# A planned attention-and-gate kernel: due times worked back from TensorE, one block fewer in plain float32, one tap a block by DMA

## The chip, the cores and the metric

The kernel runs on one core of one Trainium2 chip. The metric is the device time of one execution, in microseconds (us). The engines are called PE (TensorE, the matrix engine), DVE (VectorE), ACT (ScalarE), POOL (GpSimd) and SP (SyncE, which only issues DMAs here).

## The reference

Attention without a softmax, then a gated projection, all in float32:

```python
batch, n_heads, seq, head_dim = (8, 12, 448, 64)

def _attn_ref(q, k, v):
    scores = scale * np.matmul(q, k.transpose(0, 1, 3, 2)) - np.log(S)
    attn = 1.0 / (1.0 + np.exp(-scores))
    return np.matmul(attn, v)

def _moe_ref(x, w_val, conv_w, w_out):       # x: batch, seq, 768, the heads side by side
    for k in range(5):
        gate_pre += conv_w[k] * xp[:, k:k + S, :]   # xp: x with 4 zero tokens ahead
    gate = 1.0 / (1.0 + np.exp(-gate_pre))
    val = x @ w_val
    return gate * val @ w_out
```

## The kernel before

**Tiles.** A pair is two heads of one batch, six pairs a batch, 48 in all; a block ("two" in the code) is two pairs, 24 in all, three blocks a batch. For each pair PE makes the scores in three chunks of 128 keys (`scores`, L516), and for each block the scores of the 64 keys that are left of each head (`scores_rest`, L539). ACT takes the sigmoid (L552). Then PE multiplies with the values (`attend`, L602 for the rest, L610 for the chunks). Columns of the result are the model's 768 columns in six groups of 128, a pair each. The tokens of the first batch (number 0) are handed out over the seven others as extra columns (448 + 64 = 512), so that the projections (`product`, L753) run for seven batches: for each of six column groups 18 matmuls of 512 columns, first with `w_val`, and later with `w_out`.

**Two ways of multiplying.** In plain float32 a matmul needs no preparation. In the split way both sides are cut into a high and a low half and three products are added. For the product with the values, blocks in `WHOLE` go in plain float32: the sigmoid is written straight to SBUF as `a_single`. The other blocks are split: after the sigmoid, which is left in PSUM, ACT writes a scaled float16 copy (L367, tile `a`) and DVE subtracts it from the PSUM tile (L563); the values are scaled by a power of two of their largest element (`vm` at L531, a small matmul with ones at L536, exponents at L544 and L573 to L577) and cut into `v_hi` and `v_lo` (L583). Score tiles lie in a ring of three in PSUM (`ps_a`), projection results in a ring of two (`ps_m`). Scores have a set of their own, `WHOLE_SCORES`, the first 15 pairs.

**The gate.** For each block of batches 1 to 7 the result `x` (L661 copies the edges, L658 takes its maximum for the scaling of its own split, `xs`) is multiplied by five taps. The first product writes `gate` (L367 on ACT or L369 on DVE). Each of the four others is either a multiply-add on DVE (L679), or a product on ACT into `tap` that a DMA issued by POOL adds into `gate` (L683). The last `ADDED` taps of each block go by DMA, in the first gated batch `ADDED_FIRST`; both column groups of a block have a product each and share the DMA. Then ACT takes the sigmoid (L685).

**Weights.** The 12 column groups of both matrices come as 64-bit words in two 32-bit halves and are converted in place (`convert`, L387, L389, L367 or L369; L412), measured (L415), summed over the partitions on PE (L421) and cut into `w_hi` and `w_lo`. Three word buffers are in flight.

**The largest x.** After a batch's last block, `x_largest` puts its column maxima on a diagonal (ACT) and spreads it over the partitions by two small matmuls (L702). These are written into the first score chunk of the block's second pair, as more matmuls ahead of the chunk's own.

**What sets the order.** All work is first listed as operations (`Plan.op`): the engines that may do it, each with a modelled cost (`ways`), a time `prio`, its inputs and outputs, and what must follow it at once (`then`). `Plan.issue` walks over a modelled clock: whenever an engine is free, it takes the ready operation with the smallest `prio`, in the order P, A, V, G, S of the engines. An operation with two ways is left to ACT if ACT is free within `AT["share"]` of the time. SP's and POOL's DMAs are listed the same way, with a modelled rate and delay. The `prio` times come from the table `AT` of some 45 numbers. The result is one fixed list, and the instructions are emitted in it, so that each engine runs its own in that order.

## Time and profile before

| | us |
|---|---|
| median of 3 runs (lowest, highest) | 579.44 (578.79, 579.93) |
| the profiled execution | 579.76 |
| its span, first to last instruction | 578.0 |
| PE busy | 571.4 |
| VectorE busy | 428.4 |
| ScalarE busy | 435.4 |
| GpSimd busy | 138.2 |

The granted clock of PE is 1.00 of full speed, 2.4 GHz, over the whole span. Busy times are the union of an engine's instructions; the end of a matmul is modelled, so that the time of a group of matmuls is better read from its start to the start of what comes next.

### The profile page before, as it was taken

The page shows a single profiled execution, that of the slowest core. Times are in us where ns is not written, and L with a number is a line of the kernel's source. Part 1 is how long each engine was busy: PE and PEld are TensorE (multiplying, and loading weights), DVE is VectorE, ACT ScalarE, POOL GpSimd, SP SyncE. Part 2 cuts the span into 40 slices and gives each one's busy share as a digit, 9 for nine tenths or more (in the row PEclk, how much of TensorE's full clock was granted, in tenths as well). Part 3 has the DMA queues.
Part 4 walks back from the last instruction along what each step waited for, and adds up shares of the span by engine and source line. Part 5 has one row for each costly group of instructions (what it writes and reads, how often), then busy time and mean ns, then how long its engine had stood idle before and what let it go on. Part 6 is the DMA issues. An engine that isn't in the chain of part 4 may idle for free.

```text
span 578.0 us, 9459 instructions
## 1 busy us (share of the span) xinstructions
PE 571.4 (99%) x3592; PEld 280.2 (48%) x3592; DVE 428.4 (74%) x693; ACT 435.4 (75%) x579; POOL 138.2 (24%) x162
## 2 busy tenths in 40 slices
PE   9999999999999999999999999999999999999997
PEld 5343334455555555545555454554545555544444
DVE  1867999899977959888598886889777886760310
ACT  5677988879888869778697878788788897862112
POOL 0000203332424222243322333223322322110000
PEclk9999999999999999999999999999999999999999
DMA  8988677757484564825657364565635663355012
GB/s 327 355 279 267 174 210 188 203 120 184 124 215 83 146 157 141 207 58 155 136 158 176 102 169 96 166 156 155 169 74 168 155 133 74 72 128 129 2 37 74
DMA packets 39310, 88.44 MB, mean 153 GB/s; under 512 B 14944, under 2 KB 20448, under 8 KB 39264
## 3 DMA queue, kind: packets, MB, share of 16 engines
q0 software_dynamic: 8640, 31.46, 29.4%
q1 hardware_dynamic: 30624, 56.37, 28.9%
q8 instruction: 28, 0.46, 0.3%
q14 instruction: 18, 0.15, 0.1%
HBM read 43.96 MB, written 12.40 MB: 98 GB/s over the span
## 4 chain that ended last, share of the span: by engine, by line
PE 90%; DVE 5%; ACT 3%; DMA 1%; issue 1%; ACTq 0%; DVEq 0%
PE ps_m L753 54%; PE ps_a L516 15%; PE ps_a L610 14%; PE ps_a L539 3%; PE ps_a L602 2%; DMA gate<-tap 1%; ACT a_single L552 1%; DVE x_max L658 1%; DVE gate L679 1%; PE ps_m L800 1%; DVE a L563 1%; DVE w_words L389 1%; DVE out_max L415 0%; ACT tap L367 0%; ACT a L367 0%
## 5 line engine op out<-in xcount | busy, mean ns | idle before, releaser
L753 PE MATMUL ps_m<-g,w_out_hi 128*128 128x512 f16 (+1 forms) x516 | 150.5, 374 | 0.0
L753 PE MATMUL ps_m<-xs,w_val_hi 128*128 128x512 f16 x504 | 150.1, 379 | 0.0
L552 ACT ACTIVATE ps_a<-ps_a 128x896 f32<-128x896 f32 x112 | 99.3, 909 | 14.2 <-DVE v_exp L544 6.5
L563 DVE SCALAR_TENSOR_TENSOR a<-ps_a,a 128x896 f16<-128x896 f32 x96 | 100.8, 1082 | 7.0 <-ACT a L367 6.7
L372 POOL TENSOR_TENSOR qk_lo<-qk_src,qk_hi 128x448 fp32r<-128x448 f32 x66 | 75.2, 1151 | 119.8 <-ACT qk_hi L361 36.7
L753 PE MATMUL ps_m<-g,w_out_lo 128*128 128x512 f16 (+1 forms) x258 | 96.5, 374 | 0.0
L683 POOL DMA_DIRECT2D gate<-tap x60 | 53.5, 892 | 178.6 <-ACT tap L367 70.2
L753 PE MATMUL ps_m<-xs,w_val_lo 128*128 128x512 f16 x252 | 95.5, 379 | 0.0
L367 ACT ACTIVATE a<-ps_a 128x896 f16<-128x896 f32 x96 | 85.0, 927 | 0.2
L367 ACT ACTIVATE tap<-x,cw 128x512 f32<-128x512 f32 x120 | 82.2, 739 | 1.5 <-DMA gate<-tap 1.5
L753 PEld LDWEIGHTS <-w_out_hi 128*128 128x128 f16 x516 | 49.0, 98 | 59.6 <-issue 5.3
L753 PEld LDWEIGHTS <-w_val_hi 128*128 128x128 f16 x504 | 47.8, 98 | 61.1 <-issue 5.9
L777 DVE SCALAR_TENSOR_TENSOR y<-ps_m,y_scale,gate 128x512 f32<-128x512 f32 x42 | 29.9, 745 | 34.3 <-PE ps_m L753 34.3
L610 PE MATMUL ps_a<-a,v_hi 128*64 128x448 f16 x384 | 52.7, 354 | 0.0
L367 ACT ACTIVATE y<-ps_m,o_scale 128x512 f32<-128x512 f32 (+1 forms) x35 | 23.1, 678 | 38.0 <-PE ps_m L753 25.4
L552 ACT ACTIVATE a_single<-ps_a 128x896 f32<-128x896 f32 x56 | 48.0, 927 | 4.5 <-PE ps_a L516 4.1
L361 ACT CAST g<-y 128x512 f16<-128x512 f32 x28 | 17.2, 618 | 33.7 <-DVE y L777 32.9
L516 PE MATMUL ps_a<-qk_hi 64*128 64x448 f32 x198 | 39.8, 398 | 0.1
L753 PEld LDWEIGHTS <-w_out_lo 128*128 128x128 f16 x258 | 25.2, 98 | 29.2
L753 PEld LDWEIGHTS <-w_val_lo 128*128 128x128 f16 x252 | 24.7, 98 | 29.7
L516 PE MATMUL ps_a<-qk_single 64*128 64x448 f32 x180 | 39.0, 566 | 0.0
L610 PE MATMUL ps_a<-a_single,v_src 128*64 128x448 f32 x192 | 37.8, 543 | 0.0
(108 smaller groups left out, 752.9 us busy)
## 6 DMA issues: line engine op xcount, KB each, us to landing
gate<-tap POOLq DMA_DIRECT2D x60, 512.0 KB, 4.9
qk_src<-qk SPq DMA_DIRECT2D x33, 448.0 KB, 5.4
v_src<-vs SPq DMA_DIRECT2D x24, 448.0 KB, 4.3
out_t<-y SPq DMA_DIRECT2D x41, 224.0 KB, 3.1
qk_single<-qk SPq DMA_DIRECT2D x15, 448.0 KB, 5.9
w_words<-w_val SPq DMA_DIRECT2D x6, 768.0 KB, 8.1
w_words<-w_out SPq DMA_DIRECT2D x6, 768.0 KB, 5.4
x<-first_x SPq DMA_DIRECT2D x21, 68.0 KB, 4.2
```

What stands on the lines that cost most here:

```text
L361: nc.scalar.copy(to, x)
L367: nc.scalar.activation(to, x, AF.Copy, scale=by)
L372: engines[eng].tensor_tensor(to, x, y, op=ALU.subtract)
L516: mm(b()[:, h, :S], k()[rows, at : at + P], q()[rows, :S], start=(n == 0), stop=(n == len(terms(i)) - 1))
L539: mm(b()[to, h, :S], x[n]()[rows, CW:], x[n]()[rows, :S], start=True, stop=True)
L552: nc.scalar.activation(to, b()[:, :, :S], AF.Sigmoid, bias=-math.log(S), scale=1.0 / math.sqrt(D))
L563: op({"V": 1.0}, t + 0.5, lambda e: nc.vector.scalar_tensor_tensor(part(1), p(), A_SCALE, part(0), op0=ALU.mult, op1=ALU.subtract), [b], [ ...
L602: mm(px()[to, p, :S], v()[rows, h * D : (h + 1) * D], x(s["a"])[rows, h, at : at + S], start=(j > 0 and n == 0), stop=(j == 0 and n == len ...
L610: mm(px()[to, p, :S], v()[:, o : o + D], x(st[2 * j + p]["a", c])[:, h, at : at + S], start=(j == 0 and c == 0 and n == 0), stop=(j > 0 an ...
L683: op({"G": 1.1}, at + AT["tap_step"] * k, lambda e, tap=tap: nc.gpsimd.dma_start(g(), tap(), accum_op=ALU.add), [tap], [g], 4 * P * T * 4, "")
L753: mm(po()[:, cs], w()[:, c, :], x(k)[:, cs], start=(c == 0 and j == 0), stop=(c == NC - 1 and j == 2))
L777: op({"V": 0.66}, t + AT["y"], lambda e: nc.vector.scalar_tensor_tensor(y(), po(), y_scale()[:, m : m + 1], gate()[:, m % 2, :], op0=ALU.m ...
```

## The change

Five things change. `WHOLE` is the first 7 blocks, not 8 (14 pairs for 16), so that block 7 goes the split way. `ADDED_FIRST` and `ADDED` are 1: of each block only the last tap goes by DMA. The first step of the weight words' conversion may run on ACT too, which reads the upper 16 bits of the low half and scales them. For batch 1 the spread of the largest x stands ahead of the third score chunk, not the first. And `issue` calls the old walk (now `order`) four times: after each, `deadlines` gives each operation but PE's a new `prio`, the latest start by which PE's operations could start without a gap in the order just made; the order whose last operation ends first on the modelled clock is emitted.

```diff
-WHOLE = {*range(8)}
+WHOLE = {*range(7)}
...
+TO_THREE_BITS = 7.498 / 2**16
...
-ADDED_FIRST = 2
-ADDED = 3
+ADDED_FIRST = 1
+ADDED = 1
+
+
+TIMES = 4
...
-    def issue(self):
+    def order(self):
...
+    def issue(self):
+
+
+        best = None
+        for n in range(TIMES):
+            order = self.order()
+            end = max(o.start + o.ways[o.eng] for o in order)
+            if best is None or end < best[0]:
+                best = end, [(o, o.eng, o.start, o.end) for o in order]
+            self.deadlines(order)
+        for o, o.eng, o.start, o.end in best[1]:
+            pass
+        return [o for o, *_ in best[1]]
+
+    def deadlines(self, order):
+
+
+        nexts = [[] for _ in self.ops]
+        for o in self.ops:
+            for d in o.deps:
+                nexts[d.n].append(o)
+            for d in o.after or ():
+                nexts[d.n].append(o)
+        due, t = {}, 0.0
+        for o in order:
+            if o.eng == "P":
+                due[o.n] = t = max(t, 0.0)
+                t += o.ways["P"]
+        last = t
+        for o in reversed(order):
+            cost = min(o.ways.values()) + (o.size / self.DMA_RATE + self.DMA_DELAY if o.size else 0.0)
+            at = due.get(o.n, last)
+            for x in nexts[o.n]:
+                at = min(at, x.due - (0.0 if o in (x.after or ()) else cost + self.HOP[o.eng]))
+            o.due = at
+        for o in order:
+            if o.eng != "P":
+                o.prio = o.due
+            o.start = o.end = None
...
-        op({"V": 0.06 + 0.41 * c}, prio, lambda e: nc.vector.tensor_scalar(
-            low(), low().bitcast(U32), 2.0**-29, 7.0, op0=ALU.mult, op1=ALU.min), [], [t])
+        op({"V": 0.06 + 0.41 * c, "A": 0.1 + 0.7 * c} if w is not cw_words else {"V": 0.1}, prio, lambda e: nc.vector.tensor_scalar(
+            low(), low().bitcast(U32), 2.0**-29, 7.0, op0=ALU.mult, op1=ALU.min) if e == "V" else scaled(
+            e, low(), w().bitcast(U16)[:, :, 1], TO_THREE_BITS), [], [t])
...
-    def score(i, after=None, sums=(), then=()):
-        first, middle, last = (scores(i, c, sums if c == 0 else ()) for c in range(3))
+    def score(i, after=None, sums=(), then=(), at=0):
+        first, middle, last = (scores(i, c, sums if c == at else ()) for c in range(3))
...
-            score(2 * j + 3, None, sums, then)
+            score(2 * j + 3, None, sums, then, 2 if j == 5 else 0)
```

## Rows read from the trace of the kernel before

**Rows 1.** Page, part 1: busy time, share of the span and instructions of each engine.

```profile
PE 571.4 (99%) x3592; PEld 280.2 (48%) x3592; DVE 428.4 (74%) x693; ACT 435.4 (75%) x579; POOL 138.2 (24%) x162
```

**Rows 2.** Chain that ended last, by time: start us, us, what; float32 block, split block.

```profile
109.42 0.75 PE ps_a L602 x8
110.18 4.66 PE ps_a L610 x24
...
160.81 0.57 PE ps_a L602 x12
161.38 3.53 PE ps_a L610 x36
...
166.93 7.88 PE ps_m L753 x36
```

**Rows 3.** PE timeline: start us, us, line, operation; the matmul of a block's largest values.

```profile
134.50 0.17 PE L536 MATMUL ps_a<-vm,ones 128*128 128x1 bf16 x1
134.59 0.98 PE L539 MATMUL ps_a<-qk_src 64*64 64x448 f32 x8
```

**Rows 4.** PE timeline before 142 us; in brackets idle time before and its releaser.

```profile
45.42 0.98 PE L539 MATMUL ps_a<-qk_single 64*64 64x448 f32 x8 [0.30 <-ACT a_single L552]
...
63.32 2.53 PE L516 MATMUL ps_a<-qk_single 64*128 64x448 f32 x12
...
74.69 2.80 PE L516 MATMUL ps_a<-qk_single 64*128 64x448 f32 x12
...
78.51 0.22 PE L702 MATMUL ps_a<-diagonal,ones 128*128 128x64 bf16 x2 [0.91 <-ACT diagonal L367]
...
81.68 0.59 PE L539 MATMUL ps_a<-qk_single 64*64 64x448 f32 x2 [0.39 <-ACT a_single L552]
...
139.91 0.36 PE L516 MATMUL ps_a<-qk_hi,qk_lo 64*128 64x448 f32 x2
140.11 0.36 PE L516 MATMUL ps_a<-qk_lo,qk_hi 64*128 64x448 f32 x2
140.58 0.47 PE L516 MATMUL ps_a<-qk_hi 64*128 64x448 f32 x2
```

**Rows 5.** Timeline of all engines at 76 to 79 us: the maximum and the diagonal.

```profile
76.62 1.21 DVE L658 TENSOR_REDUCE x_max<-x 128x2 f32<-128x1024 f32 x1
...
78.06 0.40 ACT L367 ACTIVATE diagonal<-eye,x_exp 128x128 bf16<-128x128 bf16 x1
```

**Rows 6.** Busy time of each engine in two stretches (header: the columns).

```profile
core 0: us, PE busy (x) PEld busy (x) DVE busy (x) ACT busy (x) POOL busy (x), PEclk, DMA share, GB/s
...
74.00:112.00 38.00, 36.69 (x203) 15.31 (x200) 35.78 (x68) 33.37 (x46) 9.41 (x12) 1.00 0.77 197
...
142.00:500.00 358.00, 358.00 (x2378) 184.33 (x2377) 291.12 (x450) 296.68 (x397) 109.04 (x118) 1.00 0.57 139
```

**Rows 7.** Groups of instructions over the span: busy us, mean ns | idle before.

```profile
L563 DVE SCALAR_TENSOR_TENSOR a<-ps_a,a 128x896 f16<-128x896 f32 x96 | 100.8, 1082 | 7.0 <-ACT a L367 6.7
...
L367 ACT ACTIVATE a<-ps_a 128x896 f16<-128x896 f32 x96 | 85.0, 927 | 0.2
L367 ACT ACTIVATE tap<-x,cw 128x512 f32<-128x512 f32 x120 | 82.2, 739 | 1.5 <-DMA gate<-tap 1.5
...
L683 POOL DMA_DIRECT2D gate<-tap x60 | 53.5, 892 | 178.6 <-ACT tap L367 70.2 <-DVE gate L679 29.6 <-ACT y L367 21.5
...
L387 DVE TENSOR_SCALAR w_words<-w_words 128x768 int32<-128x768 uint32 x12 | 7.5, 625 | 11.2 <-DMA w_words<-w_val 11.2
```

**Rows 8.** Groups of VectorE from 74 to 112 us.

```profile
L679 DVE SCALAR_TENSOR_TENSOR gate<-x,cw,gate 128x512 f32<-128x512 f32 x9 | 6.6, 742 | 0.0
...
L583 DVE SCALAR_TENSOR_TENSOR v_lo<-v_src,v_exp,v_hi 128x896 f16<-128x896 f32 x1 | 1.2, 1152 | 0.4 <-ACT v_hi L367 0.4
...
L531 DVE TENSOR_REDUCE vm<-v_src 128x1 bf16<-128x896 f32 x1 | 1.1, 1074 | 0.0
```

**Rows 9.** Who waited for whom over the span: us, times, longest us.

```profile
ACT x L367 <- PE ps_a L610: 27.0, 16, 2.5
```

More of the change, by code (lines that the diff above doesn't have):

```diff
@@ L17 @@
 I16 = mybir.dt.int16
+U16 = mybir.dt.uint16
 I64 = mybir.dt.int64
@@ L124 @@
 class Op:
-    __slots__ = ("ways", "prio", "emit", "deps", "n", "start", "end", "eng", "after", "size", "port", "then")
+    __slots__ = ("ways", "prio", "emit", "deps", "n", "start", "end", "eng", "after", "size", "port", "then", "due")
     def __init__(self, n, ways, prio, emit, size, port):
@@ L823, in score @@
         for f in then:
-            f(st[i]["ps", 0])
+            f(st[i]["ps", at])
         for c in range(3):
```

## The prediction

> **What bounds the kernel now.** I read the page's busy shares first. TensorE (PE) is busy for 99% of the span, VectorE (DVE) 74%, ScalarE (ACT) 75% [rows 1]. A busy share alone can hide bubbles, so next I read the chain that ended last in order of time. The reader is to see that from 142 us on it is made of PE pieces alone, each starting where the one before it ends, and that equal work takes equal time: one projection group of 36 matmuls takes 7.88 us at every place, one split attention-times-values takes 0.57 + 3.53 us [rows 2]. The table of stretches says the same: between 142 and 500 us PE is busy for 358.00 of 358 us, while DVE has 291 and ACT 297 [rows 6]. So after 142 us only the amount of PE work counts, and no other engine's saving can be seen in the time.
>
> Before 142 us it is different. The PE timeline has gaps there: 0.30 us at 45.4, 0.91 at 78.5, 0.39 at 81.7; two more delays lie inside pieces, seen in their lengths: 2.80 us where the same group takes 2.53, so 0.27 us at 74.7, and a step of 0.47 us at 140.1 where its like before it in the pattern take 0.20, so another 0.27 [rows 4]. Together 2.14 us. That is all that a better order of the other engines could win, whatever it does. The stretch that makes them is crowded: from 74 to 112 us DVE is busy 35.78 of 38 us and ACT 33.37 [rows 6].
>
> The head (30 warming matmuls, first load) and the tail (last eviction and store) are not touched.
>
> **The change, part by part.**
>
> One block fewer in plain float32 (WHOLE from 8 to 7 blocks of two pairs; the block with number 7). On PE the block's product with the values takes 0.75 + 4.66 us in float32 and 0.57 + 3.53 us as three float16 products [rows 2]: 5.41 - 4.10 = 1.31 us saved. The split form also needs one matmul with the largest values, which takes 134.59 - 134.50 = 0.09 us [rows 3]. Net -1.22 us. This lies on PE at 110 us, and everything behind it is a PE chain, so it comes off the end in full.
>
> What that costs elsewhere: seven score tiles of the block now need, after the sigmoid, a scaled copy on ACT (0.93 us each) and a subtraction on DVE (1.08 us each) [rows 7]: 6.5 us more on ACT and 7.6 us more on DVE. The block's values need a maximum (1.07 us), a low half (1.15 us) [rows 8], some 0.6 us of small exponent steps, and a high half of about 1 us on either engine. In all about 10.4 us on DVE and 7.5 us on ACT. All of it falls due between 80 and 112 us, where the block is multiplied.
>
> One tap a block by DMA (ADDED_FIRST 2 to 1, ADDED 3 to 1). The 3 blocks of batch 1 lose one DMA tap each, the 18 of batches 2 to 7 two each: 39 software DMAs of 60 go, each of which held GpSimd for 0.89 us, and 78 tap products of 0.74 us leave ACT [rows 7] and come back as 78 multiply-adds of 0.74 us on DVE [rows 8], in sum 58 us moved from one engine to the other. GpSimd's own work besides is the low halves of q, k and a few g and some memsets, so it only gets freer. After 142 us DVE has 67 us free of 358 [rows 6] and PE waits for nothing; an operation that may go on either engine is given to DVE only while ACT is taken, and ACT is relieved by as much as DVE is loaded. I cost it at nothing there; the cover is the 67 us free on DVE (18 blocks with 4 products of 0.74 us, 53 us, fall there at most, which fill it to 96% if nothing moves over) and the 61 us free on ACT plus what the taps leave. Were that cover gone, the evictions of the two projection buffers would be late first, and each late eviction stops PE. Before 120 us, for batch 1's gates, 6 products move: 4.5 us to DVE, as much from ACT.
>
> Weight words: the first of three conversion steps may now run on ACT. The trace of before has no such operation. The nearest ACT row of that size takes 0.93 us [rows 7], DVE takes 0.63 [rows 7]; strided 16-bit reading could double ACT's, or cost nothing. It is a choice, not a must, and lies beside PE's work: I take it as neutral, with 0.3 us either way in the range.
>
> The move of the column spread (the small matmuls that take the largest x of batch 1 over all partitions, from the first to the third score chunk). Before, PE came to them at 77.6 and waited until 78.51 for the diagonal on ACT, which waited for the maximum on DVE (76.62 to 77.83) [rows 4, 5]. Two of the three chunks of a group of 2.53 us [rows 4] now stand ahead, 1.69 us, more than the wait of 0.91. So this wait goes, -0.91 us, with 0.78 us to spare.
>
> Orders made anew. The order on every engine is static: the plan lists the operations with a modelled clock, and each engine runs its list as written. Now a due time is worked back for each operation from the time at which PE needs its result, the list is made again, four times in all, and the one with the earliest modelled end is kept. SP's loads and stores and GpSimd's subtractions are sorted by the same times, so the loads of weights fall behind loads of q, k and v that are due sooner. The other four delays (0.30 + 0.27 + 0.39 + 0.27 = 1.23 us) are of the kind that it can remove: at 45.4 and 81.7 PE waits for a sigmoid on ACT [rows 4], and ACT and DVE had work in hand that PE wanted later. At best all go, at worst they stay. I take 1.0 us as gone.
>
> New waits from the crowding. The added work before 112 us is 10.4 + 7.5 = 17.9 us on DVE and ACT together (the taps only change sides); from 74 to 112 us both together have 2.2 + 4.6 = 6.8 us free [rows 6]. If nothing could be put off, 11.1 us are left over, half of it on each engine, and PE would be late by 5.6 us. If enough can be put off, 0. Of the nine tap multiply-adds in that stretch [rows 8] several belong to gates whose projection groups come on PE only after 112 us, and so do the taps of batch 2 on ACT and the preparation of the last output weights; I estimate some 15 us of such work on both engines, a fifth of the 69 us that they do there [rows 6]. With 6.8 + 15 us of room against 17.9 that is nearer to full cover than to none: 0.6 us is what I take.
>
> Sum: -1.22 - 0.91 - 1.0 + 0.6 = -2.5 us. The profiled execution took 579.76 us, its span 578.0 and 1.76 around it; 579.76 - 2.5 = 577.2. The median of the runs, 579.44, is 0.32 below the profiled one, so 576.9.
>
> Not all idle time is usable. Over the whole span ACT stood 27.0 us, 16 times, before the copy of a block's result out of PSUM, waiting for PE while later sigmoids were queued behind that copy [rows 9]. The Trainium skill (Perfetto Trace Analysis, section Tensor Engine Instruction (MATMUL, LD_WEIGHTS)) says that ACT, DVE and GpSimd are strict FIFOs: an operation that waits holds all behind it. It speaks against this change, since a list made with modelled durations then pays for every error of the model; if for that reason none of ACT's free time were usable, an estimate by this rule puts PE 2.3 us later and the time at 579.2. The trace agrees with the rule in these 16 waits, but after 142 us they cost PE nothing.
>
> **The rivals.**
>
> (a) The order wins nothing: the same waits come back at other places, or the first order, by the old times, is the one kept. Then only the PE work counts, and each old wait goes for a new one of its size or up to double: 579.44 - 1.22 = 578.2, and up to 2.2 more, 580.4; say 579. For it: the DVE row of 74 to 112 us, 94% full before the change. Against it: the waits of before are few and small, and the biggest is removed by the move.
>
> (b) VectorE becomes the bound between 74 and 120 us. The place is the split of block 7's score tiles: the subtraction on DVE frees the PSUM tile, and three tiles are all there are, so a late subtraction stops the scores that follow. It decides from the point where less than 9 of the 17.9 us can be put off: then over 17.9 - 6.8 - 9 = 2.1 us are left, 1 us of PE, which eats what the order saves. With ACT's 4.6 us unusable, as in the waits of [rows 9], and 7.5 of the 15 us put off, 17.9 - 2.2 - 7.5 = 8.2 us are left. Shared by both engines that is 4.1 us of PE, 579.44 - 1.22 - 0.91 + 4.1 = 581.4; with all of it on DVE 585.5; say 582.5, nearer to the shared one. For it: DVE's added 10.4 + 4.5 us against 2.2 us free. Against it: the work that isn't due.
>
> (c) All old waits go and no new one comes: 579.44 - 1.22 - 2.14 = 576.1; under this the change has nothing to win save hidden delays of less than 0.5 us, so 575.6 is the floor.
>
> **How the numbers follow.** The forecast, 576.9, with waits between 0 and 2.2 us left over (576.1 to 578.2), has 0.55, the floor case (c) among it with 0.15; rival (a), 578.2 to 580.4, 0.22; rival (b), above 580.4, 0.20; something below 575.6, 0.03. A measurement of this kernel tells about 0.2% (1.2 us) from no change: below 578.3 is faster, above 580.6 slower. Faster 0.59, the same 0.21, slower 0.20. For 8 in 10 the range leaves out the far half of (b) and the few below the floor: 575.6 to 582.0.
>
> **What would show it.** PE's chain of the block at 110 us: 0.57 + 3.53 us instead of 0.75 + 4.66 (right for the first term). The spread's matmuls without a gap before them (right for the second). PE gaps before 142 us: their sum below 1.2 us is right for the order; gaps of a microsecond before scores or value products between 80 and 125 us, released by a DVE subtraction, would show (b). 358 of 358 us busy after 142 us again, with DVE at about 90% or flexible work gone over to ACT; any gap before a projection group there, released by an eviction, would prove the tap step wrong. The number of software DMAs must be 21. What would make the prediction wrong most easily is a model whose durations are off in the crowded stretch: the list is static, so it can't give way.

## The result and the profile after

The changed kernel takes 581.21 us (median of 11 runs, 580.46 to 583.22) against 579.44 for the kernel before on the same chip (11 runs, 578.79 to 580.10). The ratio is 1.0041, with a 95% interval of 1.0030 to 1.0052: slower by 0.4%, where 576.9 us was forecast. Four of the eleven executions are a group of their own: 582.9 to 583.2 us at a mean granted clock of 0.996, the other seven 580.5 to 581.3 at 0.999 or 1.000; the profile below is one of the seven (580.56 us, span 578.8). So the medians lie 1.8 us apart and the two profiled executions 0.8: the one before was 0.32 above its median, this one 0.65 below. Line numbers are 46 or 47 higher than before: the subtraction L563 is now L610, the projection L753 is L800, the scores L516 are L563.

Busy shares, from the page, as in [rows 1]; under it two groups of instructions that answer to [rows 7]:

```profile
PE 569.1 (98%) x3609; PEld 280.7 (48%) x3609; DVE 453.3 (78%) x735; ACT 425.4 (74%) x552; POOL 115.2 (20%) x129
...
L610 DVE SCALAR_TENSOR_TENSOR a<-ps_a,a 128x896 f16<-128x896 f32 x102 | 107.0, 1082 | 10.5 <-ACT a L413 10.5
...
L730 POOL DMA_DIRECT2D gate<-tap x21 | 18.6, 887 | 126.9 <-ACT ps_a L599 24.4
```

PE is busy for 2.3 us less than before and the span is 0.8 us longer: PE is rid of the work that it was to lose, and waits instead. (About 1.1 of the 2.3 us is block 7's product; 1.0 is the head, below.) There are 21 software DMAs and 102 subtractions, as the change says.

The table of stretches, as in [rows 6]:

```profile
core 0: us, PE busy (x) PEld busy (x) DVE busy (x) ACT busy (x) POOL busy (x), PEclk, DMA share, GB/s
74.00:112.00 38.00, 37.00 (x231) 17.08 (x229) 37.98 (x63) 34.08 (x46) 9.97 (x11) 1.00 0.46 128
112.00:142.00 30.00, 28.07 (x191) 14.81 (x190) 29.28 (x57) 27.48 (x36) 7.32 (x6) 1.00 0.36 106
142.00:240.00 98.00, 97.33 (x650) 49.83 (x649) 90.45 (x144) 81.72 (x108) 24.18 (x28) 1.00 0.42 109
240.00:500.00 260.00, 260.00 (x1725) 133.93 (x1724) 223.90 (x349) 200.64 (x260) 62.94 (x63) 1.00 0.34 93
```

From 74 to 112 us VectorE is busy for 37.98 of 38 us, before it was 35.78. PE loses 1.00 us there, 1.93 us between 112 and 142 us, 0.67 between 142 and 240, and nothing from 240 to 500. Who PE waited for, over the whole span (us, times, longest; left out is the 1.1 us before its first matmul, which the kernel before has too):

```profile
PE ps_a L563 <- DVE a_rest L610: 2.6, 2, 1.9
...
PE ps_a L749 <- ACT diagonal L413: 0.6, 1, 0.6
PE ps_a L583 <- DVE vm L578: 0.4, 1, 0.4
PE ps_a L586 <- ACT a_single L599: 0.3, 1, 0.3
```

The first line is two waits with one releaser, the subtraction of a split block's rest tile, which frees a PSUM tile of the ring of three for the scores that follow. This is the PE timeline at the first of them; block 7 is ahead of it, now as three float16 products:

```profile
107.51 0.56 PE L649 MATMUL ps_a<-a_rest,v_hi 64*64 64x448 f16 x8
...
108.18 0.57 PE L657 MATMUL ps_a<-a,v_hi 128*64 128x448 f16 x4
...
111.71 0.47 PE L563 MATMUL ps_a<-qk_hi 64*128 64x448 f32 x2
...
112.22 0.36 PE L563 MATMUL ps_a<-qk_lo,qk_hi 64*128 64x448 f32 x2
114.51 0.47 PE L563 MATMUL ps_a<-qk_hi 64*128 64x448 f32 x2 [1.93 <-DVE a_rest L610]
...
115.02 0.37 PE L563 MATMUL ps_a<-qk_lo,qk_hi 64*128 64x448 f32 x2
115.23 0.36 PE L563 MATMUL ps_a<-qk_hi 64*128 64x448 f32 x2
```

From start to start, block 7 takes 0.67 + 3.53 us (before 0.75 + 4.66, [rows 2]). Then the step from one score matmul to the next takes 114.51 - 112.22 = 2.29 us, where the same step takes 115.23 - 115.02 = 0.21: 2.08 us lost. What VectorE and GpSimd did meanwhile, from their timelines:

```profile
110.09 1.91 DVE L436 TENSOR_SCALAR w_words<-w_words 128x768 int16<-128x768 int16 x2
111.77 1.68 DVE L418 TENSOR_TENSOR g<-y,g 128x512 f16<-128x512 f32 x1
113.38 1.08 DVE L610 SCALAR_TENSOR_TENSOR a_rest<-ps_a,a_rest 128x896 f16<-128x896 f32 x1
...
111.06 1.85 POOL L418 TENSOR_TENSOR g<-y,g 128x512 f16<-128x512 f32 x1 [0.97 <-ACT g L407]
```

The subtraction that PE wants stands behind the low half of a `g` that PE wants later. That low half took 1.68 us, and GpSimd made another low half beside it. The 23 of its kind on VectorE after 142 us take 0.70 on average:

```profile
L418 DVE TENSOR_TENSOR g<-y,g 128x512 f16<-128x512 f32 x23 | 16.0, 698 | 0.2
```

The second wait is built alike and comes 125 us later. The lines show the high half of an `xs` on VectorE, two low halves of q and k on GpSimd, then the chain that follows on VectorE and ScalarE, and what PE lost:

```profile
226.69 3.38 DVE L415 TENSOR_SCALAR xs<-x,x_exp 128x1024 f16<-128x1024 f32 x1
...
227.11 2.39 POOL L418 TENSOR_TENSOR qk_lo<-qk_src,qk_hi 128x448 fp32r<-128x448 f32 x2
...
236.57 0.14 DVE L591 TENSOR_SCALAR v_exp<-ps_a 128x1 int32<-128x1 int32 x1
...
236.74 0.90 ACT L599 ACTIVATE ps_a<-ps_a 128x896 f32<-128x896 f32 x1 [1.78 <-DVE v_exp L591]
...
238.62 1.09 DVE L610 SCALAR_TENSOR_TENSOR a_rest<-ps_a,a_rest 128x896 f16<-128x896 f32 x1 [1.47 <-ACT a_rest L413]
...
238.73 0.36 PE L563 MATMUL ps_a<-qk_lo,qk_hi 64*128 64x448 f32 x2
239.77 0.47 PE L563 MATMUL ps_a<-qk_hi 64*128 64x448 f32 x2 [0.68 <-DVE a_rest L610]
```

3.38 us where the other three of its kind on VectorE take about 0.75 (minimum 736 ns, median 746 of the four). VectorE runs without a gap from there to the exponent step at 236.57; the sigmoid on ScalarE waits 1.78 us for that step, the rest subtraction for the copy behind the sigmoid, and PE for the subtraction: its step takes 239.77 - 238.73 = 1.04 us, 0.84 over the usual 0.2, and PE goes on 9.7 us behind the end of the long operation (230.07).

Where the span's +0.8 us comes from: block 7 and its small matmul -1.12; waits that are new, 2.08 at 112 us, 0.84 at 239 and 0.42 at 80; waits that are gone, 0.33 of the spread's, 0.39, 0.27 and 0.27 of [rows 4]; so waits +2.1. The tail is 0.65 longer: from the start of the last matmul to the end of the span 4.05 us before, 4.70 after. The head is 1.0 shorter, by chance (last section). Together +0.6; the rest is in small pieces.

### The profile page after: what moved, and what is told of

It reads as the page before. It is cut to its first block, busy times and chain, and to the rows that moved or that the text cites. A ratio compares the mean times of both kernels' runs of the same rounds, so it can differ in the third digit from the quotient of the medians.

```text
span 578.8 us, 9418 instructions
## 1 busy us (share of the span) xinstructions
PE 569.1 (98%) x3609; PEld 280.7 (48%) x3609; DVE 453.3 (78%) x735; ACT 425.4 (74%) x552; POOL 115.2 (20%) x129
## 4 chain that ended last, share of the span: by engine, by line
PE 85%; DVE 10%; ACT 2%; issue 1%; DMA 1%; ACTq 0%; DVEq 0%
PE ps_m L800 53%; PE ps_a L563 14%; PE ps_a L657 12%; PE ps_a L586 3%; PE ps_a L649 2%; DVE a L610 2%; DVE gate L726 1%; DVE xs L779 1%; DVE w_words L436 1%; DVE xs L415 1%; ACT a_single L599 1%; DMA w_words<-w_out 1%; PE ps_m L847 1%; DVE a_rest L610 1%; DVE x_max L705 0%
## 5 line engine op out<-in xcount | busy, mean ns | idle before, releaser
L800 PE MATMUL ps_m<-g,w_out_hi 128*128 128x512 f16 (+1 forms) x516 | 150.5, 374 | 0.2 <-ACT y L413 0.2
L800 PE MATMUL ps_m<-xs,w_val_hi 128*128 128x512 f16 x504 | 150.1, 379 | 0.0
L610 DVE SCALAR_TENSOR_TENSOR a<-ps_a,a 128x896 f16<-128x896 f32 x102 | 107.0, 1082 | 10.5 <-ACT a L413 10.5
L418 POOL TENSOR_TENSOR qk_lo<-qk_src,qk_hi 128x448 fp32r<-128x448 f32 x66 | 78.7, 1224 | 176.1 <-DVE qk_hi L409 120.9
L599 ACT ACTIVATE ps_a<-ps_a 128x896 f32<-128x896 f32 x119 | 105.0, 906 | 11.3 <-DVE v_exp L591 5.9
L800 PE MATMUL ps_m<-g,w_out_lo 128*128 128x512 f16 (+1 forms) x258 | 96.5, 374 | 0.0
L800 PE MATMUL ps_m<-xs,w_val_lo 128*128 128x512 f16 x252 | 95.5, 379 | 0.0
L726 DVE SCALAR_TENSOR_TENSOR gate<-x,cw,gate 128x512 f32<-128x512 f32 x126 | 91.4, 744 | 0.0
L413 ACT ACTIVATE a<-ps_a 128x896 f16<-128x896 f32 x102 | 89.8, 928 | 0.1
L800 PEld LDWEIGHTS <-w_out_hi 128*128 128x128 f16 x516 | 49.0, 98 | 59.9 <-issue 5.6
L800 PEld LDWEIGHTS <-w_val_hi 128*128 128x128 f16 x504 | 47.8, 98 | 61.1 <-issue 5.9
L407 ACT CAST g<-y 128x512 f16<-128x512 f32 x38 | 23.6, 620 | 51.3 <-DVE y L824 51.0
L413 ACT ACTIVATE y<-ps_m,o_scale 128x512 f32<-128x512 f32 (+1 forms) x43 | 28.2, 683 | 40.7 <-PE ps_m L800 26.9
L599 ACT ACTIVATE a_single<-ps_a 128x896 f32<-128x896 f32 x49 | 41.9, 928 | 3.7 <-PE ps_a L563 3.1
L730 POOL DMA_DIRECT2D gate<-tap x21 | 18.6, 887 | 126.9 <-ACT ps_a L599 24.4
L563 PE MATMUL ps_a<-qk_hi 64*128 64x448 f32 x198 | 40.0, 400 | 2.6 <-DVE a_rest L610 2.6
L800 PEld LDWEIGHTS <-w_out_lo 128*128 128x128 f16 x258 | 25.2, 98 | 29.2
L800 PEld LDWEIGHTS <-w_val_lo 128*128 128x128 f16 x252 | 24.7, 98 | 29.7
L563 PE MATMUL ps_a<-qk_single 64*128 64x448 f32 x180 | 37.6, 552 | 0.0
L563 PE MATMUL ps_a<-qk_hi,qk_lo 64*128 64x448 f32 x198 | 36.3, 362 | 0.0
```

Of the source, the lines that this page charges most:

```text
L407: nc.scalar.copy(to, x)
L413: nc.scalar.activation(to, x, AF.Copy, scale=by)
L418: engines[eng].tensor_tensor(to, x, y, op=ALU.subtract)
L563: mm(b()[:, h, :S], k()[rows, at : at + P], q()[rows, :S], start=(n == 0), stop=(n == len(terms(i)) - 1))
L599: nc.scalar.activation(to, b()[:, :, :S], AF.Sigmoid, bias=-math.log(S), scale=1.0 / math.sqrt(D))
L610: op({"V": 1.0}, t + 0.5, lambda e: nc.vector.scalar_tensor_tensor(part(1), p(), A_SCALE, part(0), op0=ALU.mult, op1=ALU.subtract), [b], [ ...
```

## The experiments

Three readings of the waits stood against each other. Theory A: the order of the list is bad in single places; each place can be mended alone, and the gains add. Theory B: VectorE is too full between 74 and 112 us as a whole; a wait mended in one place comes back in another. Theory C: VectorE and GpSimd share an access to SBUF, single operations of VectorE are stretched beside GpSimd's, and these make the waits. For the spread of the times, theory 1 puts it on the moment at which TensorE's clock rises in the head, theory 2 on a clock that falls again after a long gap.

In the edits, `move(n, x)` takes operation n out of the list that the plan made and puts it ahead of operation x; with 1 behind it, it puts it behind x. Nothing else in the list changes. Edits are against the changed kernel (`after`). The name in brackets is the run's.

**The changed kernel again (`after_again`).** No edit.

> The changed kernel once more, unedited. In its first eleven executions 7 took 580.5 to 581.3 us and 4 took 582.9 to 583.2 with a lower mean granted clock. Theory 1 (the head): TensorE's clock goes up at a different moment of the first microseconds from execution to execution, and an execution of the longer kind has the first score groups at the lower level for some 4.6 us more, which costs 2.3 us; its waits after 10 us are the same. Theory 2 (the gap): the longer kind comes from the wait of 1.9 us at 112 us, after which the clock falls. Both kinds should be seen again; a profile of the longer kind would have its low clock before 10 us (theory 1) or after 112 us (theory 2).

Measured: 581.31 us (580.79 to 583.44, 7 runs), ratio 1.0037 (1.0022 to 1.0053). Two of the seven are of the longer group (583.44 and 583.18, clock 0.996). The wait at 112 us is there again, 1.90 us. The head's 24 first score matmuls took 5.27 us here and 4.71 in the first profile of the same kernel, which is theory 1's part. In all profiles they differ by 1.1 us at most, and the longer group takes some 2 us more. No execution of that group was profiled.

**Block 8's rest subtraction ahead of the low half (`rest_first`).**

```diff
+    move(673, 557)
```

> The changed kernel with its list kept but for one place: on VectorE the subtraction of block 8's rest tile, which frees the score tile for which TensorE waits at 112 us, stands ahead of the low half of g, which stood ahead of it. Theory A (the order of the list): the wait of 1.93 us falls by the 1.5 us of the low half that stood in front, to 0.3 to 0.6 us, and the time by 1.2 to 1.6 us. Theory B (VectorE is too full as a whole): VectorE has no free time before 116 us, so the work put back stops TensorE a little later; the wait moves, and the time falls by less than 0.5 us. Theory 2 of the gap expects the longer kind of executions to be gone, theory 1 of the head expects as many of them.

Measured: 580.37 us (579.39 to 581.22, 11 runs), ratio 1.0016 (1.0007 to 1.0025), none of the longer group. The wait at 112 us in two parts, from the PE timeline of this kernel:

```profile
114.14 0.47 PE L563 MATMUL ps_a<-qk_hi 64*128 64x448 f32 x2 [0.35 <-DVE a_rest L610]
115.49 0.47 PE L563 MATMUL ps_a<-qk_hi 64*128 64x448 f32 x2 [0.47 <-ACT x L413]
```

1.93 us became 0.35, and 0.47 came up behind it, released by ScalarE. So this place made most of the wait, and some late work was hidden behind it: the time fell by 0.8 us, less than theory A's 1.2 to 1.6 and more than B's 0.5. The move did a second thing. The subtraction now runs beside GpSimd's low half at its usual length (1.09 us), and VectorE's low half, behind it, takes 0.67 us for 1.68. So 1.0 of the 1.68 us that stood in front was theory C's.

**The high half of xs behind two subtractions (`xs_later`).**

```diff
+    move(1091, 1087, 1)
```

> The changed kernel with its list kept but for one place: on VectorE the high half of xs at 226.7 us, which took 3.38 us beside two of GpSimd's subtractions where the same operation takes some 0.8 alone, stands behind two subtractions that read PSUM. Theory C (the two engines' shared access): the operation takes at most 1.6 us there, the wait of 0.68 us and the longer step at 238 us go, and the time falls by 0.7 to 0.95 us. Rival (VectorE is late there anyway): the operation is as long in its new place or the wait stays, and the time is the same.

Measured: 580.26 us (579.38 to 582.41, 10 runs), ratio 1.0014 (1.0003 to 1.0025). The same operation in its new place, on VectorE's timeline:

```profile
229.44 0.88 DVE L415 TENSOR_SCALAR xs<-x,x_exp 128x1024 f16<-128x1024 f32 x1
```

0.88 us for 3.38; the exponent step comes at 234.95 for 236.57, ScalarE's sigmoid behind it has no gap, the rest subtraction starts at 237.01 for 238.62, and PE's gap at 239 us is gone; PE is busy for 358.00 of 358 us after 142. The same instruction on the same data, moved by 3 us, costs a quarter. That is theory C for this place: it is not the amount of work that made the wait, since that is the same.

**Both moves (`both_moves`).**

```diff
+    move(673, 557)
+    move(1091, 1087, 1)
```

> Both moves in one list. If theories A and C hold the two savings add, 1.9 to 2.5 us, and the time of the shorter kind is 578.2 to 578.9 us, just under the kernel before. If theory B holds it is 0.7 to 1.4 us.

Measured: 579.14 us (578.67 to 579.96, 11 runs), ratio 0.9998 (0.9989 to 1.0007), none of the longer group. The two savings add up to 2.1 us and bring the kernel to the time of the one before, not below it. Theories A and C as far as they go; they had expected 578.2 to 578.9.

**Eight moves (`all_moves`).** The move of `xs`, and seven more, for each wait that was left: the small maximum of the spread, block 7's maximum of the values and the rest subtraction ahead of weight steps on VectorE; the diagonal ahead of a gate product, the rest copy ahead of a `g`, block 7's result ahead of a weight conversion and a sigmoid ahead of a weight's high half on ScalarE.

```diff
+    move(1091, 1087, 1)
+    move(522, 439)
+    move(523, 504)
+    move(594, 440)
+    move(295, 364, 1)
+    move(672, 565)
+    move(673, 488)
+    move(676, 489)
```

> The changed kernel's list with eight places moved, no work added or left out: the high half of xs at 227 us as in the run before; at 77 us the largest x ahead of a weight conversion on VectorE and the diagonal ahead of a gate product on ScalarE; the maximum of block 7's values ahead of a weight conversion; at 44 us a sigmoid ahead of a weight's high half; at 112 us the scaled copy and the subtraction of block 8's rest ahead of the cast of g and of a weight conversion, and the copy of block 7's result ahead of a weight conversion. Theory A (the order of the list makes the waits, there is room on the engines): the waits at 45, 78, 80, 113 and 115 us, 2.1 us together in the list with two moves, fall by 1.3 to 2.1 us and no new one of over 0.3 us comes: 577.0 to 577.9 us, 0.2 to 0.35% under the kernel before. Theory B (the engines are too full): the work that is pushed back stops TensorE elsewhere before 145 us, and the time stays within 0.5 us of the list with two moves, 578.6 to 579.6.

Measured: 580.62 us (580.08 to 582.03, 11 runs), ratio 1.0024 (1.0015 to 1.0033). The waits of this kernel and its crowded stretch:

```profile
PE ps_a L563 <- DVE a_rest L610: 2.1, 2, 1.2
...
74.00:112.00 38.00, 37.63 (x231) 16.86 (x229) 37.94 (x62) 33.29 (x45) 9.24 (x10) 1.00 0.43 127
```

In the stretch PE gained 0.63 us (37.63 for 37.00); behind it the rest subtraction is late again, by 1.22 us at 113 and 0.87 at 140. At 113 us it is no longer in the wrong place: VectorE even stands still for 0.31 us before it, for ScalarE's copy. The whole chain is late. The exponent step that opens it (L591) starts 1.11 us ahead of PE's next score chunk (111.45 against 112.56), where in the changed kernel it is 2.34 us ahead (109.37 against 111.71). This is theory B: VectorE has 0.06 us free in the stretch, and what is put forward there puts something else back. A was right for two places and wrong as a way on.

**The rest subtraction still later (`rest_later`).** Behind two weight steps more.

```diff
+    move(673, 490, 1)
```

> The changed kernel's list with the subtraction of block 8's rest moved the other way, behind two steps of weight conversion of 0.9 us: TensorE's wait at 112 us should grow from 1.9 to 3.6 us and the time by 1.8 us, to 582.4 to 583.2 us for the shorter kind. Theory 2 (the gap takes the clock): the longer kind, some 2.3 us above it, is seen in most of the executions rather than in a quarter, and a profile of it has a stretch of half the clock after the gap. Theory 1 (the head): the longer kind is as rare as before or rarer, and where it is seen the low clock lies before 10 us.

Measured: 584.9 us (584.23 to 586.04, 4 runs), ratio 1.0102 (1.0085 to 1.0119). First the gap on PE, then a table of stretches around it (columns as above; the third value from the right is the granted clock):

```profile
116.46 0.47 PE L563 MATMUL ps_a<-qk_hi 64*128 64x448 f32 x2 [3.65 <-DVE a_rest L610]
...
112.80:117.20 4.40, 0.75 (x10) 0.70 (x10) 4.40 (x6) 2.47 (x3) 0.32 (x1) 1.00 0.85 238
117.20:120.70 3.50, 3.50 (x14) 1.46 (x11) 2.49 (x7) 3.32 (x5) 0.00 (x0) 0.51 0.01 2
```

A gap of 3.65 us, and from 117.2 to 120.7 us a clock of 0.51, that is 1.2 GHz for 2.4, with PE busy all the time. 1.7 us more of gap cost 4.0 us (584.9 against 580.9, the middle of the seven). All four executions have a mean clock of 0.994 to 0.997. Theory 2 holds for a gap of this size.

**The added multiply-adds cut (`taps_narrow`).** Of batch 1, the six multiply-adds that came back from DMA are cut to the first of eight segments; the rest of that tap is left out.

```diff
+        c1 = lambda k: 1 if f == 1 and k == KT - 2 else SEGS
...
-                        part(), x()[:, p, :, HALO - k : HALO + SL - k], w(p, k), part(), op0=ALU.mult, op1=ALU.add),
+                        part()[:, :c1(k), :], x()[:, p, :c1(k), HALO - k : HALO + SL - k], w(p, k), part()[:, :c1(k), :], op0=ALU.mult, op1=ALU.add),
```

> The changed kernel, its list unchanged, with the six multiply-adds that batch 1's gates got on VectorE cut to the first of eight segments: the rest of that tap is left out. It takes some 3.6 us from VectorE between 55 and 112 us. Theory B (too full): the wait at 112 us falls by at least 1 us. Theory A (order alone): VectorE reaches the low half of g and the subtraction earlier by what was cut, unless it waits for ScalarE's copy at 111.8 us; the wait falls by 0.2 to 1.5 us, and the ones at 78 and 80 us, which stand behind single operations, by under 0.2.

Measured: 580.11 us (one execution). The wait at 112 us fell to 0.61, which is B's "at least 1 us" and within A's range too. VectorE is still busy for 37.73 of 38 us: it fills the place of what was cut with what came after. What changed is how early it is: the exponent step (L591) starts 3.65 us ahead of PE's scores, for 2.34. So here the busy share of the stretch does not tell the wait; the lead tells it better. Two of the six cuts lie before 68 us, and the waits of 0.6 at the spread and 0.4 at 80 us stayed.

**The split's subtractions cut (`split_narrow`).** Block 7's seven subtractions work on 16 of 448 columns, and the high halves are multiplied in the place of the low ones, so that PE's work stays.

```diff
+        n = 16 if s in (st[14], st[15], two[7]) else S
...
-            part(1), p(), A_SCALE, part(0), op0=ALU.mult, op1=ALU.subtract), [b], [a], port="")
+            part(1)[:, :, :n], p()[:, :, :n], A_SCALE, part(0)[:, :, :n], op0=ALU.mult, op1=ALU.subtract), [b], [a], port="")
```

> The changed kernel, its list unchanged, with the seven subtractions of block 7's split on VectorE cut to 16 of 448 columns; TensorE multiplies the high halves twice in their place, so that its work is the same and the low halves of the probabilities are left out. It takes some 6.5 us from VectorE between 84 and 109 us. Theory B: the wait at 112 us goes. Theory A: it stays as far as the subtraction still stands behind the low half of g, which itself waits its turn, 0.3 to 1.5 us.

Measured: 579.77 us (one execution). The crowded stretch of this kernel:

```profile
74.00:112.00 38.00, 36.98 (x229) 16.96 (x227) 34.08 (x64) 35.26 (x47) 9.68 (x11) 1.00 0.48 137
```

With 3.9 us of air on VectorE the same list has a wait of 0.34 us at 112, for 1.93 (A had 0.3 to 1.5, B none); the lead of the exponent step is 3.92 us, and the low half of `g` in front of the subtraction is as long as before (1.65 us). So less load alone removes most of the wait, as order alone did. The other waits of the stretch, 0.6 at the spread and 0.4 at 80 us, stayed (PE 36.98), but they come before block 7's first subtraction (85.37 us in the changed kernel), so this cut says nothing of them.

**Eight blocks in plain float32, all else changed (`whole8`).** The list is made anew.

```diff
-WHOLE = {*range(7)}
+WHOLE = {*range(8)}
```

> The changed kernel with block 7 left in plain float32 (WHOLE of 8 blocks); the list is made anew by the plan, so single waits need not lie where they lay. Theory B (VectorE too full before 116 us for block 7's split): 10 us of VectorE's and 7.5 of ScalarE's work before 112 us go, TensorE's product is 1.22 us longer, and the waits before 142 us fall from 3.3 to at most 1.5 us; the time of the shorter kind is 579.5 us or less and the longer kind is gone. Theory A alone (the lists of the due times have bad places whatever is in them): a wait of 1 us or more is seen again somewhere, and the time is 580.5 us or more.

Measured: 578.71 us (578.47 to 579.79, 10 runs), ratio 0.9992 (0.9982 to 1.0001). A second time, on another chip (`whole8_again`):

> The changed kernel with block 7 in plain float32 once more, for a narrower interval. Theory B: 578.7 us again, no execution of the longer kind, 0.05 to 0.2% under the kernel before.

Measured: 579.03 us (578.37 to 580.05, 11 runs), ratio 0.9998 (0.9989 to 1.0007). The profile of the first:

```profile
PE ps_a L563 <- ACT x L407: 0.4, 1, 0.4
PE ps_a L586 <- ACT a_single L599: 0.3, 1, 0.3
...
74.00:112.00 38.00, 37.94 (x212) 16.25 (x212) 37.02 (x69) 30.14 (x39) 8.98 (x11) 1.00 0.62 170
...
142.00:500.00 358.00, 358.00 (x2377) 183.88 (x2376) 316.48 (x485) 277.18 (x367) 88.38 (x91) 1.00 0.36 96
```

Behind the start nothing of a microsecond is left, PE is full after 142 us with one tap a block by DMA, and the time is that of the kernel before; theory B had expected 579.5 us or less. So with this list the taps, the new orders and the move of the spread are neutral together. It is not shown that block 7's split by itself makes the changed kernel slower, since the list is another one too, and `whole8_first2` below is without the split and as slow.

**Eight blocks, with two moves (`whole8_moves`).** The waits that were left (0.4 and 0.3) mended by hand: a weight's high half behind a sigmoid, the copy of block 7's result ahead of a weight conversion.

```diff
-WHOLE = {*range(7)}
+WHOLE = {*range(8)}
...
+    move(295, 364, 1)
+    move(655, 489)
```

> The same kernel with two places of its list moved on ScalarE: at 43 us a weight's high half behind a sigmoid for which TensorE waits 0.3 us, and at 112 us a weight conversion behind the copy of block 7's result, for which it waits 0.4 us. Theory A (single places of the list, with room on the engines): both waits go and nothing comes back, -0.5 to -0.7 us, 578.0 to 578.3 us. Theory B (full even so): within 0.25 us of the kernel without the two moves, or slower.

Measured: 580.03 us (579.08 to 580.62, 11 runs), ratio 1.0012 (1.0003 to 1.0020). Theory A had expected 578.0 to 578.3 us. Both waits went; others came, of which the PE timeline shows:

```profile
46.48 0.98 PE L649 MATMUL ps_a<-a_single,v_src 64*64 64x448 f32 x8 [0.36 <-ACT a_single L599]
...
140.34 0.47 PE L563 MATMUL ps_a<-qk_hi 64*128 64x448 f32 x2 [0.31 <-ACT x L413]
```

The waits moved rather than went, as B expects, but not for fullness: they are released by ScalarE, which is busy for 24.0 of 30 us from 44 to 74 and 25.9 of 30 from 112 to 142. From 44 to 142 us PE loses 0.3 us more than without the moves; why the time rose by 1.0 us is not shown.

**The old number of taps by DMA (`taps_old`).** The list is made anew.

```diff
-ADDED_FIRST = 1
-ADDED = 1
+ADDED_FIRST = 2
+ADDED = 3
```

> The changed kernel with the taps as before (the last three of each block by DMA, two in batch 1); the list is made anew. Theory B: VectorE has 4.5 us less before 112 us and 53 us less after 142 us, and the one wait after 142 us goes; the waits before 142 us are 1.5 to 2.5 us, the time 579.0 to 580.2. If the list is what counts (theory A), its modelled end, 4.2 us later than that of the changed kernel's list, shows as a slower kernel, 581.5 us or more.

Measured: 584.9 us (584.52 to 585.16, 4 runs), ratio 1.0092 (1.0077 to 1.0107). Waits and stretches:

```profile
PE ps_a L583 <- DVE x_exp L444: 3.3, 1, 3.3
PE ps_m L800 <- DVE y L824: 1.6, 1, 1.6
...
84.70:88.20 3.50, 3.50 (x18) 0.96 (x12) 3.50 (x8) 3.50 (x6) 0.97 (x2) 0.51 0.92 295
```

Here PE waits 3.3 us for an exponent step of the largest x on VectorE, and the clock falls again behind that gap. Theory B had expected 579.0 to 580.2 us, theory A 581.5 or more from the list's modelled end. A came: VectorE has more room in the stretch than in the changed kernel (busy for 36.69 of 38 us), and PE waits longer. The run says little of the taps: after 142 us PE is full with three taps by DMA and with one. It says that another list of the same plan is 3.7 us above the changed kernel's.

**Eight blocks, batch 1 with two taps by DMA (`whole8_first2`).**

```diff
-WHOLE = {*range(7)}
+WHOLE = {*range(8)}
...
-ADDED_FIRST = 1
+ADDED_FIRST = 2
```

> The changed kernel with block 7 in plain float32 and two DMA taps in batch 1 as before, so that of the change there stay the due times, one tap a block by DMA from batch 2 on, the first conversion step on either engine and the later spread. VectorE has 4.5 us less to do before 112 us than with block 7's return alone. Theory B (VectorE's fullness makes the waits): the waits before 142 us, 0.8 us in the run with block 7's return, fall further or stay, and the time is 578.0 to 578.8 us, 0.1 to 0.3% under the kernel before. If the remaining waits come from single places of the list (theory A), they are of the same size or come back elsewhere: 578.5 to 580.

Measured: 581.69 us (580.56 to 581.88, 5 runs), ratio 1.0035 (1.0021 to 1.0049). Its waits, and the operations behind two of them:

```profile
PE ps_a L563 <- DVE a_rest L610: 3.3, 4, 1.3
...
96.26 3.00 DVE L415 TENSOR_SCALAR w_out_hi<-w_words,out_scale 128x768 f16<-128x768 f32 x1
...
293.33 3.37 DVE L415 TENSOR_SCALAR xs<-x,x_exp 128x1024 f16<-128x1024 f32 x1
```

There are four waits: 1.28 us at 99, and 0.68, 0.67 and 0.68 at 306, 381 and 457 us. The last three each come 9.7 to 9.8 us behind the end of an `xs` of 3.37 us beside two GpSimd subtractions (293.33, 368.79, 444.23), as at 226 us in the changed kernel. The first has such a cause too: the rest subtraction (99.18) stands right behind the high half of a weight that took 3.00 us beside two GpSimd subtractions (96.40 to 98.83), where the middle one of its kind takes 0.62. So theory C fits all four places. Theory B had expected 578.0 to 578.8 us and missed: VectorE is busy for 36.66 of 38 us, less than with block 7's split or without it, block 7 is not split, and the kernel is as slow as the changed one.

**The old due times (`old_times`).** The first of the four orders, by the table `AT`, is emitted.

```diff
-TIMES = 4
+TIMES = 1
```

> The changed kernel with one order only, the first, by the old table of times; all else as changed. It says what the due times are worth with these parts: the plan's own clock puts this list 24.7 us behind the one that was kept. If the plan's clock is right about large differences, 595 to 606 us; if the old table is as good as the due times, 579 to 583.

Measured: 610.87 us (2 runs), ratio 1.0541 (1.0520 to 1.0562), with waits of 10.4, 5.5 and 4.7 us on VectorE. The forecast was 595 to 606. Part of it is the clock: the granted clock is 0.84 from 74 to 112 us and 0.80 from 112 to 142. So with the parts of the change the due times are worth 30 us; the table was made for another load. With the parts of the kernel before, the plan's own modelled ends (579.8 for the first order, 582.8 for the best of the others) would keep the first, so the due times alone change nothing there; that was not run.

## Why the prediction was wrong, step by step

- *PE's work, -1.22.* Right: 0.67 + 3.53 us for 0.75 + 4.66, -1.12 with the small matmul.
- *Added work on the other engines.* Right in amount. Of the 17.9 us, only 2.20 + 0.71 = 2.9 us shows in the stretch ([rows 6] and the table above). So 15 us left it, as estimated, but not all by being put off: until 74 us the two engines together are busy for 4.6 us more than in the kernel before, all of it on ScalarE, and some 10.4 us went behind 112 us. Of four low halves of `g` one is left in the stretch, of three last conversion steps and three maxima of weights one each.
- *The weight words.* Right: six of twelve first steps went to ScalarE, and one takes 0.93 us, no more than its other operations of that size.
- *Taps at nothing after 142 us.* Right for the load: VectorE is at 314 of 358 us, 88%, and `whole8` has 358.00 of 358 on PE with the same taps. Wrong by 0.84 us at one place, and in `whole8_first2` at three, for a reason that the sum had not: an `xs` beside two GpSimd subtractions.
- *The spread, -0.91.* Only 0.33 came. The working kept the maximum and the diagonal where they stood before and let PE come 1.69 us later. In the new list a weight step (0.55 us) stands ahead of the exponent on VectorE and a gate product (0.73) ahead of the diagonal on ScalarE, so these came later too:

```profile
76.82 0.55 DVE L433 TENSOR_SCALAR w_words<-w_words 128x768 int32<-128x768 uint32 x1
77.28 0.15 DVE L743 TENSOR_REDUCE x_exp<-x_max 128x1 f32<-128x6 f32 x1
...
77.24 0.73 ACT L413 ACTIVATE gate<-x,cw 128x512 f32<-128x512 f32 x1
77.85 0.41 ACT L413 ACTIVATE diagonal<-eye,x_exp 128x128 bf16<-128x128 bf16 x1
```

- *The order, -1.0.* 0.93 of the 1.23 came: 0.39, 0.27 and 0.27 are gone, and 0.30 stayed (now at 44 us). But 0.42 is new at 80 us, before block 7's maximum of the values, and counts with the next step.
- *New waits from the crowding, +0.6.* This is the step that failed: 2.08 + 0.84 + 0.42 = 3.3 us. It set room against work as amounts. The amounts fitted; but they fitted by filling VectorE to 37.98 of 38 us, and there differences between the modelled clock and the chip came out at PE. At 112 us three came together. On the plan's clock PE comes to the tile at 114.0 us, on the chip it was there at 112.4. The low half took 1.68 us where the plan has 0.6. And the list has the low half ahead of the subtraction because the copy that the subtraction needs would come 0.26 us after VectorE is free: the plan fills that with 0.6 us of other work rather than wait, though the subtraction's due time is the earlier one.
- *Head and tail not touched.* The tail is longer by 0.5 to 0.65 us in six profiles of the changed kernel's list, its edits and `whole8` (4.54 to 4.71 us for 4.05), and not in `taps_old` and `whole8_first2` (4.07 and 4.05). In the six, SyncE pauses 0.33 to 0.35 us between its last two store issues, in the others 0.05 at most. Why it does is not shown.

Rival (b) is what happened, in its place and with its sign: a PE gap released by the subtraction that frees a score tile, at 112 us. Its price was too high (2.1 us of waits there, not 4.1) and its point of decision was wrong: more than 9 of the 17.9 us could be put off, and the waits came all the same. Its reason, VectorE's fullness, is shown for this one wait: with less work on VectorE and the same list it falls to 0.61 and 0.34 us, and in the eight moves the chain is late again. It is not the only reason. The subtraction's place in the list and the stretched low half (1.0 us) are as large, and lists with more room on VectorE wait for 3.3 us (`taps_old`) and 1.28 us (`whole8_first2`). And (b) had no term for the shared access, which makes the wait at 239 us by itself.

The prediction's last sentence named the weak point, a static list with durations that are off in the crowded stretch; the sum did not price it. By the rule that the prediction quotes from the Trainium skill (Perfetto Trace Analysis, section Tensor Engine Instruction (MATMUL, LD_WEIGHTS)), with ScalarE's free time unusable, PE would be 2.3 us later. The waits grew by 2.1 us, and that this is near is luck: ScalarE's free time did stay unused, 3.9 us of 38 after 4.6 before, but the two large waits come out of VectorE's queue, where the operations in front were at work: it was idle for 0.02 us of the stretch.

What stays open: whether a list with air for the subtractions exists that keeps block 7's 1.1 us. Of the kernels run none is clearly under the time of the kernel before; both moves and eight blocks equal it.

## What to carry to other kernels

When work moves to a helper engine, look at the stretch in which it falls due and ask how far ahead of the main engine the helper stays, not only whether the amounts fit: in a fixed list on a full engine (37.98 of 38 us) a wrong duration or order can come out as a wait of the main engine. Look also for operations that are far above their usual length beside another engine's: here such an operation stands ahead of both large waits of the changed kernel and of all four in `whole8_first2`. Saving on the main engine makes it come earlier to the very places where the helper got later, so 1.1 us saved there can cost 2 us. A list that is made anew is another draw: here lists of nearly the same work lay between 578.7 and 584.9 us, wider than any single part of the change, so a part is judged only with its list looked at.

## What the runs showed of the hardware

**VectorE beside GpSimd.** The `xs` high half (float32 to float16, 128x1024, both in SBUF) takes 0.75 us alone and 3.37 to 3.38 us in the four places shown, where two GpSimd subtractions ran; it ended 0.57 us after the last of these (230.07 against 229.50). The low half of `g`, two operands in SBUF, took 1.68 us for 0.68 and ended 0.54 us after GpSimd's. In the changed kernel 11 VectorE operations take over 0.3 us more than the middle one of their kind, and all 11 overlap a GpSimd subtraction; of the 119 subtractions out of PSUM 63 overlap one too, and none takes more than 1.09 us. The kernel before has 15 such operations, all beside GpSimd's, and PE waits for none of them after 142 us: a stretched operation costs time only where PE's next need stands behind it. The Trainium skill (SBUF — State Buffer, section Who interferes with whom) says that VectorE and GpSimd share a pair of ports as an exclusive lock, and that whoever comes second is blocked, not slowed. The lengths agree roughly: the rest of GpSimd's work and then the operation's own. It also says that the first to issue gets the pair; the record of `xs` begins 0.42 us ahead of GpSimd's and it was the one that waited, so a start in the trace doesn't tell who came first. The plan's own model lets the two engines use this access one after the other; in the traces the two overlap where one of them is late against the plan.

**The clock after a gap.** Behind PE gaps of 3.3 and 3.65 us the granted clock is 0.51 for 3.5 us although PE is busy again; 8 of 8 executions of these two kernels have a mean clock of 0.994 to 0.997. Of the three runs with the gap of 1.9 us (`after`, `after_again`, `xs_later`), 7 of 28 executions have a mean of 0.996 or 0.997 and take some 2 us more; one of 16 with gaps of 1.2 and 1.3 us; none of the 54 of `rest_first`, `both_moves`, `whole8` (both times) and `whole8_moves`, which have no gap of a microsecond. That these 7 had the same half-clock stretch is inferred from the mean: none of them was profiled. The Trainium skill (TensorE: Matmul & The Clock Gate, section Part 1: The HAM clock gate) has the two levels, 1.2 and 2.4 GHz, and the return to the lower one after idle time; the two profiled gaps of over 3 us agree.

**The head.** The first 24 score matmuls take 4.71 to 5.78 us in seven profiles, of kernels that don't differ there, as the clock rises at another moment each time. The traces' clock records have the full level from 4.0 us behind the first instruction in the changed kernel, from 5.6 in its second profile and from 6.1 in the kernel before, where the 24 matmuls take 4.71, 5.27 and 5.56 us: about a microsecond of spread that no change of a list explains.
